# Seven half-block products for the second feed-forward product of nine token pairs

## The chip, the core and the metric

The kernel runs on one core of one Trainium2 chip. TensorE (PE in the profile; PEld is its weight load, which overlaps the matmuls) multiplies into eight PSUM banks; VectorE (DVE), ScalarE (ACT) and GpSimd (POOL) do the elementwise work; SyncE (SP) issues most DMAs. Each engine takes its instructions strictly in the order in which the program lists them for it and waits on semaphores for the others. The metric is the device time of one execution in microseconds. The kernel before took 181.5 us, the median of three runs (181.38 to 181.68).

## The reference

A gated outer-product recurrence runs over 768 time steps for 4 batches and 8 heads of width 48; its result, 3072 tokens of width 384, goes through a feed-forward layer of width 2048. All arrays are float32 outside the kernel.

```python
def _attn_ref(q, k, v, f_logit):                      # 4, 8, 768, 48
    f = 1.0 / (1.0 + np.exp(-f_logit))
    for t in range(S):
        state = f[:, :, t, :, None] * state + np.einsum('bhd,bhe->bhde', k[:, :, t], v[:, :, t])
        y[:, :, t] = np.einsum('bhd,bhde->bhe', q[:, :, t], state)

def _moe_ref(x, w_in, w_out):                         # 3072x384, 384x2048, 2048x384
    h = x @ w_in
    g = h * (1.0 / (1.0 + np.exp(-h)))
    return g @ w_out
```

## The kernel before

**Tiles.** The sequence is cut into chunks of 128 tokens, six for each batch, 24 in all. Two chunks form a pair (`PAIRS`). Pairs 0 to 3 (form T) hold the first two chunks of one batch, with even and odd tokens dealt to the two tiles; pairs 4 to 11 (form N) hold the same chunk of two batches.

**Tasks.** A pair goes through a fixed set of tasks, named by two or three letters. Loads `f`, `k`, `q`, `v` come through SP. `E` and `L` (ACT) take the logarithm of the gate, `cs` (PE) sums it over the chunk, `a`, `ia`, `al` (ACT) take exponentials of the sums. `qg` and `ki` (DVE or POOL, line 341) multiply q and k by them. They are transposed, either on PE (`tq`, line 348, and a copy `qkc`) or by a DMA from SP (`qkD`, line 360). `sc` (PE, lines 369 and 373) makes the scores, `at` (DVE, line 377) masks them, `y` (PE, lines 285, 385, 389) makes the chunk's result, `d`, `sd` and `su` (PE, DVE, POOL or DVE; lines 297, 406, 410, 420) carry the state to the next chunk. `yc` copies the result out of PSUM as bf16; it is transposed into `xT` on PE (`yT`, line 397, with the copy `xc`) or by DMA (`yD`, line 401).

**The feed-forward layer.** `mi` (line 271) is one of eight parts of the first product: two blocks of 128 of the 2048 columns, three matmuls of 256 token columns for each, with the weights of `w_in_sb` as the loaded operand. For pairs 0 and 1 each part is done for one chunk at a time, with matmuls of 128 columns. `si` (ACT, line 276) takes SiLU of a part into `hT`, bf16. `mo` (line 306) is one of four parts of the second product for one chunk: four matmuls of 384 columns that accumulate in one PSUM bank, with a block of `hT` as the loaded operand and `w_out_sb` streamed. A chunk needs 16 of them. Only pair 11 does them in two halves of 192 columns. `oc` (lines 185 and 187) copies the bank into `ob`, `so` (lines 316 and 318) stores it.

**Order.** A table, `PLAN`, lists every task with its engine and the buffer that it takes. The program is emitted in that order, so the table sets the order in every engine's queue, SP's included. `idle` tasks (line 465) are matmuls of zeros that nothing reads: they stand where PE would have nothing to do at the start. `SLOTS` gives the number of buffers of each kind: six each for k, q and v, and eight PSUM banks (`pb`) for all uses. A change of activation table (line 513) is inserted wherever ACT's next task needs another one.

Of the kernel before, what the change touches and what calls it, by code (L numbers as in the profile page):

```python
# [10 lines left out]
F32 = mybir.dt.float32  # L11
BF16 = mybir.dt.bfloat16
AF = mybir.ActivationFunctionType
PSUM = bass.MemoryType.PSUM
# [19 lines left out]
SLOTS = dict(f=4, k=6, q=6, v=6, e=2, lf=3, x=5, qk=5, vb=7, qkT=4, qkTT=2, atm=4, yb=3, xT=4, hT=4, sd=2, al=6, ob=6, pb=8, st0=1, st1=1, st2=1, st3=1)  # L34
# [15 lines left out]
mi.0.1.1:P:0 si.0.3:A:1 mi.0.1.0:P: mi.0.5.1:P: si.1.5:A: ki.3.0:G: mi.0.0.0:P:6 si.0.1:A: mi.0.6.0:P:5 mi.0.0.1:P: su.1.1:G:0 mi.0.7.1:P:4 si.0.0:A:  # L50
mi.0.7.0:P: si.0.2:A: mi.0.6.1:P: ki.3.1:G: mi.1.1.0:P: si.0.6:A: mi.1.7.0:P:0 tq.3.0:P:6 mi.1.7.1:P: qkc.3.0:A:1 mi.0.4.0:P:2 tq.3.1:P:5 si.1.7:A:
mi.0.4.1:P: f.4.0:S:1 mo.0.0.0:P:6 qkc.3.1:A: mo.0.1.0:P:0 si.1.1:A: mi.1.6.1:P:5 si.0.5:A: mi.1.6.0:P: si.1.2:A: mo.1.1.0:P:7 si.1.6:A: mo.0.1.1:P:
si.0.4:A: si.0.7:A: sc.3.1:P:3,1 sc.3.0:P:5,2 at.3.1.0:V:2 vb.2.0:A:4 mo.0.1.2:P: at.3.1.1:V: mo.1.1.1:P: at.3.0.0:V:3 mo.0.0.1:P: q.4.0:S:4
mo.0.1.3:P: vb.3.0:V:5 mo.1.1.2:P: vb.3.1:V:6 oc.0.1:V:0 mo.1.1.3:P: at.3.0.1:V: v.5.0:S:4 mo.0.0.2:P: vb.2.1:V:2 v.5.1:S: oc.1.1:V:1 d.2:P:4,3
so.1.1:G: y.2:P:1,5 su.2.0:V:0 v.4.0:S:5 d.3:P:0,2 E.4.0:A:0 sd.2.1:V:0 y.3:P:7,4 yc.3.0:V:1 yi.2.1:P: mo.1.0.0:P:3 L.4.0:A:1 yc.2.1:V:2 yT.3.0:P:7
su.3.0:V:0 mo.1.0.1:P: yc.2.0:V:0 v.8.1:S:0 mo.0.0.3:P: sd.3.1:V:1 yT.2.1:P:5 oc.0.0:A:2 cs.4.0:P:0 k.4.0:S:4 xc.2.1:V:2 yi.3.1:P: a.4.0:A:2 so.0.0:G:
mo.1.0.2:P: ia.4.0:A:1 q.4.1:S: xc.3.0:A:3 yT.2.0:P:1 mo.1.0.3:P: xc.2.0:V: E.5.0:A:1 k.6.1:S:5 mi.2.2:P:2 al.4.0:A:4 cs.4.1:P:6 mi.2.3:P:5 al.4.1:A:5
a.4.1:A:3 q.5.0:S:5 L.5.0:A:2 mi.2.7:P:7 k.5.1:S:0 yc.3.1:A:1 mi.2.4:P:1 ia.4.1:A:0 ki.4.0:G:1 q.5.1:S: mi.2.5:P:0 oc.1.0:A:3 vb.4.0:G:3 yT.3.1:P:4
mi.2.0:P:6 xc.3.1:V: su.2.1:G:0 mi.3.6:P:3 si.2.3:A:2 mi.3.1:P:4 qg.4.0:V: si.2.7:A: k.4.1:S: su.3.1:G:0 si.2.5:A: mi.3.7:P:5 si.3.1:A:3 f.6.0:S:2
mi.2.6:P:7 vb.5.1:A:0 si.3.7:A: d.4.0:P:0 v.4.1:S: mi.2.1:P:4 sd.4.0:V:0 si.2.6:A: qg.4.1:V:2 tq.4.0:P:5 si.2.4:A: mi.3.2:P:0 si.2.1:A: k.7.0:S:1  # L60
si.2.0:A: mi.3.0:P:7 ki.4.1:G: qkc.4.0:A:0 cs.5.1:P:1 mi.3.5:P:4 qkD.4.1:S:1 si.3.0:A: mo.2.1.0:P:6 si.2.2:A: si.3.5:A: sc.4.0:P:5,7 v.7.0:S:1
# [485 lines left out]
```

## Time and profile before

| | |
|---|---|
| device time, median of three runs | 181.5 us (181.38 to 181.68) |
| span of the profiled execution, first to last instruction | 179.2 us |
| PE busy | 170.5 us, 2042 matmuls |
| ACT busy | 132.7 us, 251 instructions |
| DVE busy | 79.7 us, 166 instructions |
| POOL busy | 61.6 us, 106 instructions |
| granted TensorE clock | 1.000 |
| HBM read and written | 25.17 MB and 4.72 MB |

The profile is one execution. The device time of that execution is not recorded apart; its span is 2.3 us shorter than the median, and those 2.3 us lie before the first and after the last instruction. "Busy" is the time in which at least one instruction of an engine runs. A group of instructions is shown with its line, engine, operation, the tiles that it writes and reads, its shape and its count, then its busy time, the mean duration of one, and the idle time of its engine just before it. The chain of waits starts at the last instruction and goes back, at each step, to what released it.

### The profile page before, as it was taken

The numbers are of one execution on the slowest core, as the hardware profiler recorded it, in microseconds if no ns is written. First come the engines' busy times: TensorE is split into PE (matmuls) and PEld (weight loads), VectorE is DVE, ScalarE is ACT, GpSimd is POOL, SyncE is SP. The second block draws the span as 40 slices with busy tenths as digits, with TensorE's granted clock in tenths as the row PEclk, the third lists the DMA queues.
The fourth block names the chain that finished last, engine by engine and source line by source line (L and its number), as shares of the span: only waits on it lengthen the run. The fifth ranks groups of instructions, "written<-read, shape, count | busy, mean of one in ns | idle before, by whom it ended". The sixth has DMA issues, their size and how long they took to land.

```text
span 179.2 us, 4981 instructions
## 1 busy us (share of the span) xinstructions
PE 170.5 (95%) x2042; PEld 129.0 (72%) x2044; DVE 79.7 (44%) x166; ACT 132.7 (74%) x251; POOL 61.6 (34%) x106
## 2 busy tenths in 40 slices
PE   6769989999999999999999999999999999999993
PEld 2345779975788866778678877875876786788782
DVE  7078994008821246456673703342335747500002
ACT  3989983895289999999967558988796991178410
POOL 6036995000274004554044170636303592000010
PEclk9999999999999999999999999999999999999999
DMA  6999999999999799998478998994994496320043
GB/s 159 324 325 325 240 204 207 199 187 190 242 230 212 92 208 221 168 241 144 84 145 170 188 210 141 252 263 103 179 251 94 97 190 215 88 70 0 0 150 117
DMA packets 109366, 31.91 MB, mean 178 GB/s; under 512 B 103536, under 2 KB 108768, under 8 KB 109344
## 3 DMA queue, kind: packets, MB, share of 16 engines
q1 hardware_dynamic: 104464, 25.60, 70.2%
q0 software_dynamic: 4880, 6.00, 15.7%
q8 instruction: 16, 0.26, 0.6%
q14 instruction: 6, 0.05, 0.1%
HBM read 25.17 MB, written 4.72 MB: 167 GB/s over the span
## 4 chain that ended last, share of the span: by engine, by line
PE 77%; ACT 9%; DVE 4%; DMA 3%; SPq 2%; issue 1%; POOL 1%; DVEq 0%
PE pb L306 32%; PE pb L271 32%; ACT hT L276 4%; DMA q<-in_q_dram 3%; PE pb L373 2%; SPq L241 2%; PE pb L385 2%; PE pb L348 2%; PE pb L389 2%; DVE qk L341 2%; ACT L513 1%; DVE atm L377 1%; PE pb L331 1%; PE pb L397 1%; DVE st L420 1%
## 5 line engine op out<-in xcount | busy, mean ns | idle before, releaser
L306 PE MATMUL pb<-w_out_sb,hT 128*128 128x384 bf16 (+1 forms) x416 | 70.4, 314 | 0.2 <-ACT hT L276 0.2
L271 PE MATMUL pb<-xT,w_in_sb 128*128 128x256 bf16 (+1 forms) x672 | 68.9, 257 | 0.0
L271 PEld LDWEIGHTS <-w_in_sb 128*128 128x128 bf16 x672 | 56.6, 98 | 7.5 <-issue 0.3
L276 ACT ACTIVATE hT<-pb 128x512 bf16<-128x512 f32 x96 | 51.8, 617 | 12.4 <-PE pb L271 12.0
L306 PEld LDWEIGHTS <-hT 128*128 128x128 bf16 x416 | 37.7, 98 | 18.7 <-ACT hT L276 0.4
L377 DVE TENSOR_TENSOR atm<-pb,triu 128x512 bf16<-128x512 f32 x32 | 20.6, 684 | 20.5 <-PE pb L373 17.8
L336 ACT ACTIVATE x<-pb 128x384 f32<-128x384 f32 x48 | 22.1, 508 | 1.5 <-PE pb L331 1.4
L420 POOL TENSOR_TENSOR st<-sd,al 48x192 bf16<-48x192 f32 x32 | 16.6, 518 | 18.7 <-PE pb L385 12.1
L341 POOL TENSOR_TENSOR qk<-q,x 128x384 bf16<-128x384 f32 x11 | 11.3, 1025 | 31.9 <-ACT x L336 14.5
L513 ACT ACT_TABLE_LOAD x15 | 19.2, 1283 | 0.3
L185 ACT COPY ob<-pb 128x384 f32<-128x384 f32 (+1 forms) x15 | 6.8, 453 | 12.6 <-PE pb L306 12.6
L377 DVE TENSOR_TENSOR atm<-pb,mask 128x512 bf16<-128x512 f32 x16 | 10.2, 685 | 12.4 <-ACT hT L276 11.1
L187 DVE COPY ob<-pb 128x384 f32<-128x384 f32 (+1 forms) x11 | 5.8, 535 | 22.2 <-PE pb L306 22.2
L318 POOL DMA_DIRECT2D out_dram<-ob x8 | 4.6, 578 | 28.4 <-ACT ob L185 24.8
L316 POOL DMA_DIRECT2D out_dram<-ob x14 | 7.6, 548 | 19.6 <-DVE ob L187 15.9
L341 DVE TENSOR_TENSOR qk<-q,x 128x384 bf16<-128x384 f32 x13 | 7.6, 593 | 13.7 <-ACT x L336 13.7
L248 ACT ACTIVATE e<-f 128x768 f32<-128x768 f32 (+1 forms) x13 | 10.4, 800 | 4.4 <-DMA f<-in_f_logit_dram 4.2
L410 DVE TENSOR_TENSOR sd<-pb,st 128x384 f32<-128x384 f32 x16 | 8.9, 554 | 10.6 <-PE pb L406 3.9
L341 POOL TENSOR_TENSOR qk<-k,x 128x384 bf16<-128x384 f32 x10 | 10.8, 1082 | 6.4 <-ACT al L278 2.0
L185 ACT CAST yb<-pb 128x384 bf16<-128x384 f32 x12 | 5.6, 479 | 9.7 <-PE pb L389 9.6
L341 DVE TENSOR_TENSOR qk<-k,x 128x384 bf16<-128x384 f32 x14 | 9.9, 710 | 0.9 <-ACT x L336 0.9
L187 DVE CAST yb<-pb 128x384 bf16<-128x384 f32 x12 | 6.6, 556 | 8.0 <-PE pb L389 5.9
(72 smaller groups left out, 157.4 us busy)
## 6 DMA issues: line engine op xcount, KB each, us to landing
f<-in_f_logit_dram SPq DMA_DIRECT2D x11, 384.0 KB, 4.7
q<-in_q_dram SPq DMA_DIRECT2D x16, 192.0 KB, 4.1
v<-in_v_dram SPq DMA_DIRECT2D x16, 192.0 KB, 3.9
k<-in_k_dram SPq DMA_DIRECT2D x16, 192.0 KB, 3.9
k<-in_k_dram SPq DMA_DIRECT2D x4, 384.0 KB, 4.8
v<-in_v_dram SPq DMA_DIRECT2D x4, 384.0 KB, 9.5
q<-in_q_dram SPq DMA_DIRECT2D x4, 384.0 KB, 4.9
w_in_sb<-in_moe_w_in_dram POOLq DMA_DIRECT2D x4, 384.0 KB, 9.5
```

The lines of the kernel that those rows point to most:

```text
L185: nc.scalar.copy(dst, src)
L187: ENG[eng].tensor_copy(dst, src)
L248: return nc.scalar.activation(e, at("f", P)[:, j * w:(j + 1) * w], AF.Exp, scale=-1.0)
L271: nc.tensor.matmul(h[:, i, cols], w_in_sb[:, kk, n * 128:(n + 1) * 128], at("xT", P)[:, kk, cols], start=(kk == 0), stop=(kk == KT - 1))
L276: return nc.scalar.activation(at("hT", P)[:, 2 * j:2 * j + 2, :], at("h", P, j).rearrange("p (n c) -> p n c", n=2), AF.Silu)
L306: nc.tensor.matmul(at("o", P, i)[:, cols], at("hT", P)[:, n, i * C:(i + 1) * C], w_out_sb[:, n, cols], start=(n == 0), stop=(n == NT - 1))
L336: nc.scalar.activation(at(kind, P, i).rearrange("p h d -> p (h d)"), at("cs", P, i)[:, 0:HD], AF.Exp, scale=1.0 if kind == "ia" else -1.0)
L341: ENG[eng].tensor_mul(at("qk", P, i)[:, j, :, 0:D], heads("qk"[j], P, i), at("ia" if j else "a", P, i))
L377: ENG[eng].tensor_mul(at("atm", P, i)[:, r], at(f"s{r}", P, i).rearrange("p (n c) -> p n c", c=C), mask[:, None, :].to_broadcast([C, NP, C]))
L410: nc.vector.tensor_add(at("sd", P, i), d_ps, prev_state(P, i))
L420: ENG[eng].tensor_mul(at("st", P, i)[lo:lo + D, :, r * D:(r + 1) * D], src[lo:lo + D, :, r * D:(r + 1) * D], al_of(P, i)[lo:lo + D, :, Non ...
L513: nc.scalar.preload_act_table_set(TABLES[mode])
```

## The change

**The second product.** For pairs 2 to 10 the product of the pair's 256 by 2048 block with the 2048 by 384 weights is split in half in all three directions and done by Strassen's scheme. `hT` is laid out chunk by chunk, so that its four blocks are (chunk, half of the 2048). The weights' four blocks are 1024 by 192.

- `wt`, five times in all: a sum or difference of two weight blocks, in bf16, on DVE (8 blocks of 192 columns, 1536 elements in each partition), into the new tiles `w_sum`.
- `hs`, four times for each pair, on DVE: sums and differences of blocks of `hT` in bf16. Numbers 1, 6 and 7 have 1024 elements in each partition, number 5 makes two sums at once and has 2048. Numbers 6 and 7 are written over a block of `hT`, number 1 into a free `qkT` buffer, number 5 into a free `qkTT` buffer.
- `ms`, seven times for each pair: eight matmuls of 192 columns. Numbers 2 to 5 go into the two halves of one PSUM bank, 6 and 7 into those of a second, 1 into half of a third.
- `cc`, `ca` and `oc`: seven of the nine `cc` copies and all 36 `ca` sums are on DVE, and of the nine `oc` copies four on DVE and five on ACT. `cc` copies a quarter out of PSUM, `ca` 0 and 1 add a quarter to it, `ca` 2 and 3 make the two diagonal quarters of the output from it, `oc` copies the two others.

Pairs 0, 1 and 11 keep the old product.

**Buffers.** k, q and v have four buffers each instead of six. The result of `E` is written over `f`, whose buffers `e` go away. `ob` holds a pair: four of them instead of six single ones. `qkT` has one buffer more.

**Order.** `PLAN` is new throughout. One pair of `tq`/`qkc` and one of `yT`/`xc` have become DMA transposes; 15 whole-chunk stores are on SP instead of 8, and 7 on POOL instead of 14 (the stores of a T pair are two DMAs each); 28 idle matmuls instead of 24, of which 21 in a row at the start instead of 11; 18 activation table loads instead of 16; on POOL one `qg` and one `ki` less and four `vb` more; on ACT four `vb` less.

```diff
-SLOTS = dict(f=4, k=6, q=6, v=6, e=2, lf=3, x=5, qk=5, vb=7, qkT=4, qkTT=2, ..., ob=6, pb=8, ...)
+SLOTS = dict(f=4, k=4, q=4, v=4, lf=3, x=5, qk=5, vb=7, qkT=5, qkTT=2, ..., ob=4, pb=8, ..., ct=2)
...
-f.2.0:S:0 k.0.0:S:0 f.0.1:S:1 f.0.0:S: E.2.0:A:0 f.1.0:S:2 L.2.0:A:0 v.1.0:S:0 q.0.0:S:0 idle.512.11::0 cs.2.1:P:0 ...
+f.2.0:S:0 f.0.1:S:1 f.0.0:S: f.1.0:S:2 v.0.0:S:0 q.0.0:S:0 E.2.0:A: E.0.1:A: L.2.0:A:0 k.0.0:S:0 L.0.1:A:1 idle.512.21::1 cs.2.1:P:0 ...
...
+    KH, W = NT // 2, d_model // 2
+    w_sum = {m: sb.tile([128, KH, W], BF16, name=f"w_sum{m}") for m in (1, 3, 4, 6, 7)}
...
+    BANK = {2: "oa", 3: "oa", 4: "oa", 5: "oa", 6: "ob2", 7: "ob2", 1: "oc"}
+    def h_sum(P, m):
+        if m == 5:
+            return at("hE", P).rearrange("p j n g s c -> p (j n g s c)").rearrange("p (u n c) -> p u n c", u=2, c=C)
+        if m == 1:
+            return at("hF", P).rearrange("p j n c -> p (j n) c")
+        return at("hT", P)[:, 1, 0:KH, :] if m == 6 else at("hT", P)[:, 0, KH:NT, :]
...
+        if kind == "wt":
+            blk = lambda r, c: w_out_sb[:, r * KH:(r + 1) * KH, c * W:(c + 1) * W]
+            x, y, op = {1: (blk(0, 0), blk(1, 1), ALU.add), 3: (blk(0, 1), blk(1, 1), ALU.subtract), 4: (blk(1, 0), blk(0, 0), ALU.subtract),
+                        6: (blk(0, 0), blk(0, 1), ALU.add), 7: (blk(1, 0), blk(1, 1), ALU.add)}[rest[0]]
+            return ENG[eng].tensor_tensor(out=w_sum[rest[0]], in0=x, in1=y, op=op)
+        if kind == "hs":
+            m = rest[1]
+            hT = at("hT", P)
+            blk = lambda u, k: hT[:, u, k * KH:(k + 1) * KH, :]
+            x, y, op = {6: (blk(1, 0), blk(0, 0), ALU.subtract), 7: (blk(0, 1), blk(1, 1), ALU.subtract), 1: (blk(0, 0), blk(1, 1), ALU.add),
+                        5: (hT[:, :, 0:KH, :], hT[:, :, KH:NT, :], ALU.add)}[m]
+            return ENG[eng].tensor_tensor(out=h_sum(P, m), in0=x, in1=y, op=op)
+        if kind == "ms":
+            m = rest[1]
+            hT = at("hT", P)
+            for n in range(KH):
+                if m == 3:
+                    x, w = hT[:, 0, n], w_sum[3][:, n]
+                elif m == 4:
+                    x, w = hT[:, 1, KH + n], w_sum[4][:, n]
+                elif m == 5:
+                    x, w = h_sum(P, 5)[:, 0, n], w_out_sb[:, KH + n, W:2 * W]
+                elif m == 2:
+                    x, w = h_sum(P, 5)[:, 1, n], w_out_sb[:, n, 0:W]
+                else:
+                    x, w = h_sum(P, m)[:, n], w_sum[m][:, n]
+                half = 1 if m in (2, 4, 6) else 0
+                first = n == 0 and m in (1, 3, 6, 7)
+                nc.tensor.matmul(at(BANK[m], P)[:, half * W:(half + 1) * W], x, w, start=first, stop=(n == KH - 1), skip_group_check=True)
+            return
+        if kind == "cc":
+            return copy(eng, at("ct", P), at("oa", P)[:, W:2 * W])
+        if kind == "ca":
+            ct = at("ct", P)
+            two = lambda x: x[:, 0:2 * W].rearrange("p (u w) -> p u w", w=W)
+            if rest[1] < 2:
+                return nc.vector.tensor_add(ct, at("oa", P)[:, 0:W] if rest[1] == 0 else at("oc", P)[:, 0:W], ct)
+            diag = at("ob", P).rearrange("p u (x w) -> p (u x) w", w=W)[:, 0:4:3, :]
+            if rest[1] == 2:
+                return nc.vector.tensor_sub(diag, ct[:, None, :].to_broadcast([C, 2, W]), two(at("oa", P)))
+            return nc.vector.tensor_add(diag, two(at("ob2", P)), diag)
...
-                e = at("e", P)[:, j * w:(j + 1) * w]
+                e = at("f", P)[:, j * w:(j + 1) * w]
...
-            return nc.scalar.activation(at("hT", P)[:, 2 * j:2 * j + 2, :], at("h", P, j).rearrange("p (n c) -> p n c", n=2), AF.Silu)
+            return nc.scalar.activation(at("hT", P).rearrange("p u n c -> p n u c")[:, 2 * j:2 * j + 2], at("h", P, j).rearrange("p (n u c) -> p n u c", n=2, u=2), AF.Silu)
```

**Three places where the order changes.** In the rows below a row names the line (of its own kernel), the operation, the tile written, the tiles read and the shape.

PE, near the end, where the products of pair 10 begin among the last `mi` of pair 11. Before (hT3 is pair 10's block, pb a PSUM bank):

```order
L306 MATMUL pb0_140<-w_out_sb_162,hT3_125 128x384
...
L271 MATMUL pb1_141<-xT3_121,w_in_sb_161 128x256
...
L306 LDWEIGHTS hT3_125
L306 MATMUL pb5_145<-w_out_sb_162,hT3_125 128x384
...
L306 MATMUL pb7_147<-w_out_sb_162,hT2_124 128x192
```

Now (hT1 is pair 10's block, hT3 pair 9's, qkT4 holds sum 1 of pair 10):

```order
L267 LDWEIGHTS hT1_116
L267 MATMUL pb5_136<-w_sum3_157,hT1_116 128x192
...
L267 MATMUL pb5_136<-w_sum4_158,hT1_116 128x192
...
L329 MATMUL pb1_132<-xT3_114,w_in_sb_154 128x256
...
L267 MATMUL pb3_134<-w_sum6_159,hT3_118 128x192
...
L267 MATMUL pb6_137<-w_sum1_156,qkT4_101 128x192
```

A chunk's sixteen matmuls of 384 columns into one bank have become runs of eight of 192 columns into halves of three banks, and products of two pairs stand among each other.

DVE, in the last third, from the masks of pairs 10 and 11 to the last copies. Before (the rows up to the end of DVE's list):

```order
L377 TENSOR_TENSOR atm_114<-pb_145,triu 128x512
L377 TENSOR_TENSOR atm_113<-pb_146,triu 128x512
L187 COPY ob_134<-pb_142 128x384
L187 CAST yb_116<-pb_144 128x384
L187 COPY ob_139<-pb_145 128x384
L187 COPY ob_137<-pb_140 128x384
L187 COPY ob_134<-pb_146 128x192
```

Now (hT_118 is pair 9's block, ct the running quarter of an output):

```order
L435 TENSOR_TENSOR atm_107<-pb_138,triu 128x512
L193 CAST yb_109<-pb_137 128x384
L250 TENSOR_TENSOR qkTT_102<-hT_118 128x2048
L275 TENSOR_TENSOR ct_143<-pb_136,ct_143 128x192
L278 TENSOR_TENSOR ob_130<-ct_143,pb_132 128x2x192
L250 TENSOR_TENSOR hT_118<-hT_118 128x1024
L275 TENSOR_TENSOR ct_144<-pb_134,ct_144 128x192
```

Where seven rows took DVE from the last masks to the end of its list, sums of blocks and of PSUM quarters now follow one another; masks and copies for `y` stand behind them in the same queue.

SP, at the very start. Before:

```order
L241 DMA f_61<-in_f_logit_dram 128x8x96
L241 DMA k_65<-in_k_dram 128x8x96
L241 DMA f_62<-in_f_logit_dram 128x4x96 x2
L241 DMA f_63<-in_f_logit_dram 128x8x96
L241 DMA v_77<-in_v_dram 128x8x96
L241 DMA q_71<-in_q_dram 128x8x96
```

Now:

```order
L299 DMA f_61<-in_f_logit_dram 128x8x96
L299 DMA f_62<-in_f_logit_dram 128x4x96 x2
L299 DMA f_63<-in_f_logit_dram 128x8x96
L299 DMA v_73<-in_v_dram 128x8x96
L299 DMA q_69<-in_q_dram 128x8x96
L299 DMA k_65<-in_k_dram 128x8x96
```

The first k goes from second to seventh DMA, and pair 0's gate and q each come one place earlier; the v that is loaded first is pair 0's and no longer pair 1's.

178 lines of the change are left out of this document (97 added, 81 removed).

## The prediction, made before the changed kernel had run

> **What bounds the kernel now.** I read the busy shares first, then the slices, the chain of waits, and two stretches by engine.
>
> ```profile
> PE 170.5 (95%) x2042; PEld 129.0 (72%) x2044; DVE 79.7 (44%) x166; ACT 132.7 (74%) x251; POOL 61.6 (34%) x106
> ...
> PE   6769989999999999999999999999999999999993
> ...
> DVE  7078994008821246456673703342335747500002
> ACT  3989983895289999999967558988796991178410
> ...
> PE 77%; ACT 9%; DVE 4%; DMA 3%; SPq 2%; issue 1%; POOL 1%; DVEq 0%
> ...
> 60.00:70.00 10.00, 9.97 (x102) 6.84 (x99) 3.70 (x7) 9.94 (x18) 2.01 (x3) 1.00 1.03 174
> ...
> 120.00:140.00 20.00, 20.00 (x194) 14.20 (x192) 6.79 (x13) 16.43 (x31) 6.51 (x9) 1.00 0.77 157
> ```
>
> The two last rows are stretches: length, then busy time and count of PE, PEld, DVE, ACT, POOL. From about 27 us to 176 us PE has no gap, and the chain lies on it for 77% of the span. ACT is full only around 50 to 80 us, beside a PE that is full too. DVE is 44% busy. Time is therefore PE's work plus what PE waits. What PE's pieces cost stands in the chain (start, us, piece):
>
> ```profile
> 35.00 0.67 PE pb L271 x12
> 35.67 0.45 PE pb L348 x8
> 47.87 0.17 PE pb L397 x3
> 115.57 0.17 PE pb L385 x4
> 115.74 0.20 PE pb L389 x8
> 120.52 5.20 PE pb L306 x32
> 141.32 5.24 PE pb L271 x48
> 163.73 0.33 PE pb L306 x4
> 166.67 9.52 PE pb L306 x88
> ```
>
> Back to back, a matmul of 384 columns takes 5.20/32 = 162.5 ns, of 256 columns 5.24/48 = 109 ns, of 192 columns (the piece of four is half a `mo` of pair 11) 0.33/4 = 82.5 ns, of 128 columns 0.67/12 = 56 ns. The last piece checks the third: by the order 28 of its 88 matmuls have 384 columns and 60 have 192, so (9.52 - 28 x 0.1625)/60 = 82.8 ns.
>
> **The change on PE.** Nine pairs gave up 9 x 32 = 288 matmuls of 384 columns, 46.8 us, for 9 x 56 = 504 of 192, 41.6 us: **-5.2 us**. One `tq` (0.45) and one `yT` (0.17) leave PE: **-0.6 us**; their DMA transposes go to SP.
>
> **The start.** What ran before the first score, in time order:
>
> ```profile
> 1.37 4.37 PE L465 MATMUL pb<-zero,triu 128*128 128x512 bf16 x11 [1.37 <-POOL triu masks.py:66]
> 4.92 0.84 ACT L260 ACTIVATE lf<-e 128x768 bf16<-128x768 f32 x1
> 5.82 0.48 PE L324 MATMUL pb<-lf,tincl 128*128 128x384 bf16 x2
> ...
> 5.24 4.81 DMA q<-in_q_dram
> ```
>
> Eleven idle matmuls ended as the first logarithm did, at 5.8 us. Twenty-one end later: the ten more at the 384-column pace (512/384 x 0.1625 = 0.217 us) take 2.2 us, to 7.9 us, while the logarithm, now behind half of another exponential, ends about 0.5 us later than before. So pair 0's cumulative sums start about 1 us late. Against that q is one transfer earlier than its 10.05 us, and ACT and DVE have fewer copies ahead of it; k, now the seventh transfer, lands about where q did. I charge **0**, with 1.5 us to either side. The end (last copy, last store) is unchanged: 0.
>
> **The change on DVE.** Durations by form (busy, mean ns):
>
> ```profile
> L377 DVE TENSOR_TENSOR atm<-pb,triu 128x512 bf16<-128x512 f32 x32 | 20.6, 684 | 20.5 <-PE pb L373 17.8 <-ACT hT L276 2.6
> L341 DVE TENSOR_TENSOR qk<-k,x 128x384 bf16<-128x384 f32 x14 | 9.9, 710 | 0.9 <-ACT x L336 0.9
> L410 DVE TENSOR_TENSOR sd<-pb,st 128x384 f32<-128x384 f32 x16 | 8.9, 554 | 10.6 <-PE pb L406 3.9 <-POOL st L420 3.1 <-PE pb L397 1.7
> L187 DVE COPY ob<-pb 128x384 f32<-128x384 f32 x10 | 5.4, 552 | 22.0 <-PE pb L306 22.0
> L187 DVE CAST vb<-v 128x384 bf16<-128x384 f32 x11 | 5.1, 482 | 0.0
> L187 DVE COPY qkTT<-pb 128x1024 bf16<-128x1024 bf16 x3 | 2.0, 680 | 0.0
> L187 DVE COPY xT<-pb 128x384 bf16<-128x384 bf16 x4 | 1.4, 353 | 4.8 <-PE pb L397 4.8
> L187 DVE COPY ob<-pb 128x192 f32<-128x192 f32 x1 | 0.4, 359 | 0.2 <-PE pb L306 0.2
> ```
>
> No row has a two-input bf16 sum from SBUF, so `hs` and `wt` are bounded from both sides. By slope of the float32 rows, (684 - 554)/128 = 1.02 ns an element, 1024 elements take 1.21 us, 1536 1.73, 2048 2.25. By that of the bf16 copies, (680 - 353)/640 = 0.51 ns, they take 0.68, 0.94 and 1.20 us. I take the lower, since the type is that of the copies, and keep the upper as a rival. [...]
>
> All nine pairs: `hs` 27 x 0.68 + 9 x 1.20 = 29.2 us, `wt` 5 x 0.94 = 4.7, `ca` 18 x 0.36 + 18 x 0.554 = 16.5, `cc` 7 x 0.36 = 2.5; the output copies come out about even, and two more `qg`/`ki` add 1.1. DVE goes from 79.7 to some 134 us. That fits the whole span, but not evenly. Between pair 1's last product and the fifth product of pair 9, counted in the changed order, PE has 51 `ms` (0.66 each), 51 `mi` (0.655) and, by the small pieces shown (0.37 for a `y`, 0.17 for a `d`, about 0.35 for one `sc` of eight), 16.4 us of others: 83.5 us. In the same stretch DVE has 30 masks x 0.644 (busy over count) = 19.3, 20 short and 7 long `hs` = 22.0, 28 `ca` = 12.6, 6 `cc` = 2.2, and 46 others (`sd`, `yc`, `qg`, `ki`, `oc`, `vb`, one `qkc`) = 25: 81 us. **So DVE needs 97% of PE's time for two thirds of the kernel.**
>
> On top comes GpSimd. These rows are VectorE's products with two SBUF inputs (minimum/median/maximum ns), and one of them in time order beside a POOL product:
>
> ```profile
> L341 DVE TENSOR_TENSOR qk<-k,x x14: 547/550/1359, 10.6 to 141.6; 128x384 bf16<-128x384 f32 x14
> L341 DVE TENSOR_TENSOR qk<-q,x x13: 542/549/1111, 10.1 to 141.2; 128x384 bf16<-128x384 f32 x13
> ...
> 11.44 1.06 POOL L341 TENSOR_TENSOR qk<-k,x 128x384 bf16<-128x384 f32 x1 [2.04 <-ACT al L278]
> 11.56 1.36 DVE L341 TENSOR_TENSOR qk<-k,x 128x384 bf16<-128x384 f32 x1
> ```
>
> The DVE product that met POOL's ended 0.42 us after it and took 0.8 us more than the median. The means (710, 593) lie above the medians by 14 x 0.16 + 13 x 0.04 = 2.8 us over 27 products, 0.1 us each. `hs` has two SBUF inputs as well: 42 such operations in the stretch cost 4.2 us more, 85.2 us in all, 1.7 us over PE. [...] I charge **+1.8 us** as PE waiting for DVE. Its lower bound is 0 (rows that stand back to back overlap a little), its upper bound is the first rival.
>
> What is queued behind a late `hs` on DVE: masks, then `y` on PE, and the copies that free PSUM banks; a pair's product now holds three banks instead of two.
>
> **Other parts.** ACT gains two table loads and loses seven copies of `ob`, four of `vb`, one `qkc` and one `xc`: 2 x 1.28 against about 3.4 + 2.2 + 1.0 + 0.5, so it becomes lighter by some 4 us; 0 on the path, PE being full beside it. POOL has two products of 1.03 less, four casts more and eight stores less: 0. These rows price them:
>
> ```profile
> L513 ACT ACT_TABLE_LOAD x15 | 19.2, 1283 | 0.3
> L185 ACT COPY ob<-pb 128x384 f32<-128x384 f32 x12 | 5.8, 486 | 4.9 <-PE pb L306 4.9
> L341 POOL TENSOR_TENSOR qk<-q,x 128x384 bf16<-128x384 f32 x11 | 11.3, 1025 | 31.9 <-ACT x L336 14.5 <-issue 9.6 <-DVE sd L410 7.6
> L420 POOL TENSOR_TENSOR st<-sd,al 48x192 bf16<-48x192 f32 x32 | 16.6, 518 | 18.7 <-PE pb L385 12.1 <-DVE sd L410 5.2
> ```
>
> **The sum.** 179.2 - 5.2 - 0.6 + 0 + 1.8 = 175.2 us of span; with the 2.3 us that lie around it, **177.5 us** against the median of 181.5.
>
> **Rivals.** *VectorE becomes the bound* (slower). POOL reads SBUF for 24 of the stretch's 83.5 us (12 `su` of two rows of 0.52, 9 products of 1.03 to 1.08, 4 casts of about 0.5). If each of the 42 two-input operations meets it that often (28%) at the full 0.8 us, DVE needs 81 + 9.5 = 90.5 us there, 7.0 more than PE: 179.2 - 5.8 + 7.0 + 2.3 = **182.7**. It is slower than before from 89.7 us of DVE on (83.5 + 5.8 + 0.4). For it: the 97%, and masks that feed PE from the same queue. Against it: most `hs` stand several PE parts ahead of their product in the order, and the mean excess was 0.1 us.
>
> *The sums run at the float32 pace* (slower). The stretch's `hs` take 20 x 1.21 + 7 x 2.25 = 40.0 instead of 22.0 us: 18 more, so 177.5 + 18, about **195**. Against it: bf16 copies run at twice that pace.
>
> *Loads and transposes late behind stores.* SP gets fourteen more store DMAs and two more transposes.
>
> ```profile
> SPq L318 <- DVE ob L187: 14.9, 3, 12.0
> ...
> 118.70 1.83 SPq L316 DMA_DIRECT2D out_dram<-ob  x2
> ...
> qkT<-qk SPq DMA_TRANSPOSE x14, 3.5
> ```
>
> At 0.9 us each they take SP some 15 us more, a store that waits for DVE has held SP for 12 us, and k, q and v can be fetched less far ahead. One transpose (3.5 us to landing) that PE then waits for gives 177.5 + 3.5 = **181.0**.
>
> *Weight loads bound the short matmuls* (slower).
>
> ```profile
> L306 PEld LDWEIGHTS <-hT 128*128 128x128 bf16 x416 | 37.7, 98 | 18.7 <-ACT hT L276 0.4
> ```
>
> If each of the 504 took its load's 98 ns, they would need 49.4 us, 7.8 more than charged: **185.3**. The 56 ns of twelve matmuls with a load each speak against it. [...]
>
> **How the numbers follow.** Forecast 0.58; VectorE the bound 0.22; SP late 0.11; float32 pace 0.06; weight loads 0.03. The forecast's own range is 175 (start 1 us better, no waiting) to 179.5. The range to hold the time 8 times in 10 is 175.0 to 183.5: below it 0.05, above it the float32 pace, the weight loads and a quarter of the first rival, 0.14. A difference of 0.2% is about what the spread of the runs before lets one tell from none. Faster: the forecast and half of SP late, 0.64. Same: 0.04 of SP late and 0.02 of the first rival, 0.06. Slower: 0.30.
>
> **What would show it.** `ms` at 82 ns a matmul in the chain, and PE busy of some 165 us. `hs` at about 0.7 and 1.2 us; at 1.2 and 2.25 the third case has come. DVE at 130 to 138 us, with full slices from 60 to 150 us; PE gaps there that end on DVE's masks or sums, 1 to 3 us in all by the forecast, 6 or more by the first rival. PE waiting for a DMA transpose would mean SP. First scores later than 15.5 us would make the start's 0 wrong.

## The result, and the profile after

The changed kernel took **186.6 us** (median of four runs, 185.3 to 186.8) against 181.4 us before: 1.0259 times as long, 95% interval 1.0216 to 1.0303. The forecast was 177.5 us. The profiled execution took 186.75 us, its span was 185.0 us. Here and below a median is over all executions, while a ratio leaves out those that ran slow, at a lower clock throughout or more than 1.5% above the fastest of their kernel.

The page of the profile after: busy times, slices, the chain's shares, and three groups.

```profile
PE 169.2 (91%) x2253; PEld 144.5 (78%) x2253; DVE 125.2 (68%) x252; ACT 130.7 (71%) x240; POOL 54.7 (30%) x94
...
PE   7996989999999999989949959999986999999992
...
DVE  6159973574668888789946493997949589907340
...
PEclk9999999999999999999987988999999999999999
...
PE 60%; DMA 11%; ACT 10%; SPq 7%; DVE 5%; issue 4%; POOL 1%; DVEq 0%; POOLq 0%; ACTq 0%
...
L329 PE MATMUL pb<-xT,w_in_sb 128*128 128x256 bf16 (+1 forms) x672 | 73.2, 262 | 4.6 <-DMA xT<-yb 3.9
...
L250 DVE TENSOR_TENSOR qkTT<-hT 128x2048 bf16<-128x2048 bf16 x9 | 11.0, 1218 | 6.4 <-ACT hT L334 6.4
...
L250 DVE TENSOR_TENSOR hT<-hT 128x1024 bf16<-128x1024 bf16 x18 | 12.3, 690 | 0.1
```

PE's row, all nines from 27 us on before, now has a 4 at 92 us, a 5 at 106 us and a 6 at 139 us (a slice is 4.6 us), and the clock has two dents, from 92 to 102 us and from 106 to 116 us. DMA and SP's queue together, 5% of the chain before, are 18%. DVE is less busy than forecast, and its long sums take what was put for them. The holes by name, from the order of time on PE (start, length, group, idle before it and what ended that):

```profile
79.83 1.47 PE L329 MATMUL pb<-xT,w_in_sb 128*128 128x256 bf16 x12 [0.74 <-ACT hT L334]
95.64 1.00 PE L431 MATMUL pb<-qkT 48*128 48x128 bf16 x16 [2.71 <-DMA qkT<-qk]
108.42 5.76 PE L329 MATMUL pb<-xT,w_in_sb 128*128 128x256 bf16 x36 [2.19 <-DMA xT<-yb]
137.75 0.40 PE L431 MATMUL pb<-qkT 48*128 48x128 bf16 x8 [0.89 <-DMA qkT<-qk]
142.90 1.48 PE L329 MATMUL pb<-xT,w_in_sb 128*128 128x256 bf16 x12 [1.69 <-DMA xT<-yb]
```

They add up to 8.2 us; from 27 us on there is no other wait of PE over 0.2 us. Four of the five end on a DMA transposition, none on a sum of VectorE. The third row shows a second loss: 36 matmuls of 256 columns took 5.76 us, 160 ns each, where 109 ns was the pace before. The stretches around it (length; PE, PEld, DVE, ACT, POOL; granted clock; DMA share; GB/s):

```profile
108.00:111.00 3.00, 2.58 (x17) 2.02 (x18) 3.00 (x6) 0.06 (x1) 0.00 (x0) 0.73 0.92 179
111.00:114.00 3.00, 3.00 (x21) 2.31 (x20) 1.48 (x3) 1.14 (x3) 0.00 (x0) 0.70 1.08 209
114.00:117.00 3.00, 3.00 (x45) 2.44 (x43) 1.17 (x2) 2.91 (x6) 0.00 (x0) 1.00 1.01 222
```

The 0.73 and 0.70 are means over three microseconds. The trace's records of the granted clock say more exactly: 0.50 from 109.36 to 112.78 us and 1.00 on either side, and likewise 0.50 from 95.71 to 99.12 us, behind the first long hole. Each is a stretch of 3.41 us at half speed, which costs 1.7 us of TensorE's work. What makes a transposition late is best seen in the chain of waits of the same kernel (start, length, what lay on the chain):

```profile
122.46 0.67 PE pb L267 x8
123.34 0.62 SPq L374
124.00 0.59 SPq L374
124.70 1.27 SPq L418
126.02 1.26 SPq L459
...
131.25 0.79 SPq L376
132.08 1.85 DMA out_dram<-ob
133.94 3.77 DMA qkT<-qk
137.75 0.42 PE pb L431 x8
```

For ten microseconds, from 123.3 to 133.9 us, the chain does not touch PE: it goes from command to command through SP's queue, stores (lines 374 and 376), transpositions (418, 459) and loads. Then the transposition that PE needs is issued and takes 3.8 us.

### The profile page after: what moved, and what is told of

The parts are those of the page before. It is cut to its first block, busy times and chain, and to the rows that moved or that the text cites. A ratio compares the mean times of both kernels' runs of the same rounds, so it can differ in the third digit from the quotient of the medians.

```text
span 185.0 us, 5495 instructions
## 1 busy us (share of the span) xinstructions
PE 169.2 (91%) x2253; PEld 144.5 (78%) x2253; DVE 125.2 (68%) x252; ACT 130.7 (71%) x240; POOL 54.7 (30%) x94
## 4 chain that ended last, share of the span: by engine, by line
PE 60%; DMA 11%; ACT 10%; SPq 7%; DVE 5%; issue 4%; POOL 1%; DVEq 0%; POOLq 0%; ACTq 0%
PE pb L329 27%; PE pb L267 13%; PE pb L364 6%; DMA qkT<-qk 5%; PE pb L533 4%; DMA xT<-yb 3%; DVE atm L435 3%; ACT L581 3%; ACT hT L334 3%; SPq L299 3%; DMA v<-in_v_dram 2%; ACT x L394 2%; SPq L418 2%; PE pb L431 2%; SPq L374 1%
## 5 line engine op out<-in xcount | busy, mean ns | idle before, releaser
L329 PE MATMUL pb<-xT,w_in_sb 128*128 128x256 bf16 (+1 forms) x672 | 73.2, 262 | 4.6 <-DMA xT<-yb 3.9
L267 PE MATMUL pb<-w_sum,hT 128*128 128x192 bf16 x288 | 29.2, 246 | 0.0
L267 PEld LDWEIGHTS <-hT 128*128 128x128 bf16 x288 | 23.7, 98 | 0.7
L364 PE MATMUL pb<-w_out_sb,hT 128*128 128x384 bf16 (+1 forms) x128 | 18.6, 286 | 0.0
L267 PE MATMUL pb<-w_out_sb,qkTT 128*128 128x192 bf16 x144 | 15.5, 253 | 0.1
L250 DVE TENSOR_TENSOR qkTT<-hT 128x2048 bf16<-128x2048 bf16 x9 | 11.0, 1218 | 6.4 <-ACT hT L334 6.4
L364 PEld LDWEIGHTS <-hT 128*128 128x128 bf16 x128 | 11.2, 98 | 2.6
L267 PEld LDWEIGHTS <-qkTT 128*128 128x128 bf16 x144 | 12.5, 100 | 0.7 <-issue 0.4
L306 ACT ACTIVATE f<-f 128x768 f32<-128x768 f32 (+1 forms) x13 | 10.4, 809 | 2.8 <-DMA f<-in_f_logit_dram 2.8
L250 DVE TENSOR_TENSOR hT<-hT 128x1024 bf16<-128x1024 bf16 x18 | 12.3, 690 | 0.1
L533 PE MATMUL pb<-zero,triu 128*128 128x512 bf16 x28 | 9.3, 498 | 1.4 <-POOL triu masks.py:66 1.4
```

Of the source, the lines that this page charges most:

```text
L250: return ENG[eng].tensor_tensor(out=h_sum(P, m), in0=x, in1=y, op=op)
L267: nc.tensor.matmul(at(BANK[m], P)[:, half * W:(half + 1) * W], x, w, start=first, stop=(n == KH - 1), skip_group_check=True)
L306: return nc.scalar.activation(e, at("f", P)[:, j * w:(j + 1) * w], AF.Exp, scale=-1.0)
L329: nc.tensor.matmul(h[:, i, cols], w_in_sb[:, kk, n * 128:(n + 1) * 128], at("xT", P)[:, kk, cols], start=(kk == 0), stop=(kk == KT - 1))
L364: nc.tensor.matmul(at("o", P, i)[:, cols], at("hT", P)[:, i, n], w_out_sb[:, n, cols], start=(n == 0), stop=(n == NT - 1))
L533: nc.tensor.matmul(buf["pb", int(got)][:, 0:rest[0]], triu, zero[:, 0:rest[0]], start=True, stop=True, skip_group_check=True)
```

## The experiments

Medians throughout; ratios, with their 95% intervals, are to the kernel before on the same chip (181.3 to 181.7 us).

**e1: stores off SP.** The seven stores of T pairs that the change put on SP, 14 DMAs, go back to POOL's queue, at the same places.

```diff
-so.0.0:S: ... so.0.1:S: ... so.3.1:S: ... so.1.0:S: ... so.1.1:S: ... so.2.1:S: ... so.2.0:S:
+so.0.0:G: ... so.0.1:G: ... so.3.1:G: ... so.1.0:G: ... so.1.1:G: ... so.2.1:G: ... so.2.0:G:
```

> The changed kernel with the seven whole-chunk stores of the T pairs (fourteen DMAs) issued by POOL instead of SP, at the same places of the table. Theory SP (SP's queue is full from 70 to 140 us, so DMA transposes and loads leave it late and PE waits for them): SP is 9 to 14 us lighter between 95 and 133 us, the gaps after 100 us shrink, time 181 to 185. Theory DVE (VectorE's sums make PE late): 186.6, unchanged within 0.5. Theory BUF (four buffers for k, q, v instead of six let the loads start late): 185.5 to 186.6.

Measured 180.1 us (178.1 to 182.6), 0.9873 [0.979, 0.9957]: 6.5 us less than the changed kernel and now below the kernel before. From its page and its order of time on PE:

```profile
PE 166.0 (93%) x2253; PEld 142.5 (80%) x2253; DVE 126.0 (71%) x252; ACT 130.8 (73%) x240; POOL 62.7 (35%) x108
```

```profile
94.03 0.62 PE L430 MATMUL pb<-qkT 48*128 48x128 bf16 x16 [1.30 <-DMA qkT<-qk]
...
105.00 4.09 PE L328 MATMUL pb<-xT,w_in_sb 128*128 128x256 bf16 x36 [1.61 <-DMA xT<-yb]
...
136.16 1.48 PE L328 MATMUL pb<-xT,w_in_sb 128*128 128x256 bf16 x12 [0.54 <-DMA xT<-yb]
```

The same holes, smaller (4.3 us with the others from 27 us on that are over 0.2 us and wait for an engine or a DMA), and the same 36 matmuls at 4.09 us, at full clock. PE's busy time falls by 3.2 us with not one matmul fewer: that much of it had been clock, two stretches of 1.7 us. The transposition behind the first hole is issued before any T store, so its shrinking from 2.71 to 1.30 us isn't the stores' doing: the same wait is 1.41 us in e13, with the stores on SP, and 2.09 us in e11, without them. Some 3 us of the difference between these two profiles, this hole and its clock, are therefore not to be put down to the stores; but the 6.5 us are the difference of the medians, and a repetition (e16, below) gives 180.2 us again. Nor do the stores hold SP by waiting for their data: in the changed kernel's list of SP's waits none belongs to a T store.

**e8: the reverse.** The same seven stores of the kernel before go from POOL to SP, everything else as before.

```diff
-so.1.1:G: ... so.0.0:G: ... so.2.0:G: ...
+so.1.1:S: ... so.0.0:S: ... so.2.0:S: ...
```

> The kernel before with its seven T-pair stores that POOL issues (fourteen DMAs) issued by SP at the same places of the table. If such stores on SP are enough by themselves: 183 to 187, with PE gaps that end on transposes. If they harm only beside loads that come just in time (four buffers, new order): 181.4 to 182.3.

Measured 184.0 us, 1.0141 [1.0115, 1.0166]: 2.7 us more. From 27 us on its one hole over a microsecond ends on a transposition:

```profile
128.32 0.83 PE L270 MATMUL pb<-xT,w_in_sb 128*128 128x256 bf16 x6 [1.52 <-DMA xT<-yb]
```

So the stores on SP cost either kernel time, the changed one more. That this is for want of PE work that covers the transpositions is argued below.

**e2 and e10: no sums on VectorE.** The sums of `hs` and `wt` are left out, in e2 from the changed kernel, in e10 from e1.

```diff
-            return ENG[eng].tensor_tensor(out=w_sum[rest[0]], in0=x, in1=y, op=op)
+            return
-            return ENG[eng].tensor_tensor(out=h_sum(P, m), in0=x, in1=y, op=op)
+            return
```

> The changed kernel without the sums of hT blocks and of weight blocks: the 63 half-block products read the unsummed blocks, so the output is another one. VectorE loses 29 + 4.7 us of work, everything else stands. Theory DVE: 180 or less, since VectorE is then far from PE's work. Theories SP and BUF: 185 to 187, since no load, store or transpose moves.

> As e1 (the stores of pairs 0 to 3 on POOL), and with all sums of weight and activation blocks left out, so that each product takes a block as it stands; what is left out is 42 operations, 31 us of VectorE. If VectorE holds TensorE up by the 1.8 us that the prediction put for it, this comes to 178 us against e1's 180.1. If the sums cost nothing once SP is free, 180 us. If they cost as much as their removal was worth with the stores on SP, 2.4 us, 177.7 us.

e2: 184.2 us, 1.0108 [1.0039, 1.0178], 2.4 us less than the changed kernel. The page and the order of time on PE:

```profile
PE 166.9 (91%) x2253; PEld 143.0 (78%) x2253; DVE 94.6 (51%) x211; ACT 130.7 (71%) x240; POOL 52.9 (29%) x94
```

```profile
94.44 0.62 PE L423 MATMUL pb<-qkT 48*128 48x128 bf16 x16 [2.52 <-DMA qkT<-qk]
...
104.48 0.40 PE L423 MATMUL pb<-qkT 48*128 48x128 bf16 x8 [1.76 <-DMA qkT<-qk]
...
107.16 5.76 PE L321 MATMUL pb<-xT,w_in_sb 128*128 128x256 bf16 x36 [1.52 <-DMA xT<-yb]
...
141.88 1.48 PE L321 MATMUL pb<-xT,w_in_sb 128*128 128x256 bf16 x12 [2.09 <-DMA xT<-yb]
```

With 31 us taken from VectorE the kernel is still slower than before, and its waits on transpositions are at least as long in sum. The time lies between the two expectations, and the runs do not show where the 2.4 us come from; in the profiles e2 has one stretch at half clock where the changed kernel has two, which is 1.7 us. e10: 180.9 us (177.9 to 181.6), 0.9858 [0.9771, 0.9945], against e1's 180.1 us: nothing that can be told from zero, though a spread of some 4 us would hide one or two. **VectorE is not what made the kernel slower.**

**e3 and e7: the old product in the new order.** Pairs 2 to 10 get `mo` back where `ms` stood, without sums; in e3 the stores stay on SP, in e7 they are on POOL as in e1. In e3 some banks and output buffers are overwritten before their last reader has read them; in e7, where the copies `oc` of pairs 5, 6 and 7 stand in another order, they are not.

```diff
-hs.4.5:V:1 ... ms.4.3:P:0 ... ms.4.4:P: ... cc.4:V:0 ... ca.4.0:V: ... ms.4.2:P: ...
+mo.4.0.0:P:0 ... mo.4.0.1:P: ... mo.4.0.2:P: ...
```

> The changed kernel with the old second product for pairs 2 to 10 (matmuls of 384 columns at the places of the half-block products, two copies for each pair, no sums), in the new order, with the new buffers, stores and loads. PE's work is 5.2 us more, VectorE's some 50 us less. If the new order and its loads and transposes are the cause: 186 to 190. If the half-block scheme itself is (sums, three banks for each pair, weight loads): 181 to 183.

> The old second product in the new order, as before, but with the T pairs' stores on POOL. What the half-block scheme is worth where SP holds PE less: PE's work is 5.2 us more than in the changed kernel with the stores on POOL, so 183 to 185.5 if PE bounds both; 180 to 181 if both are bound by transposes or the sums take back what the products give.

e3: 185.3 us, 1.0191 [1.0127, 1.0254]. e7: 183.9 us, 1.0125 [1.0091, 1.0159]. Its page, and its longest wait in the order of time on PE:

```profile
PE 171.3 (94%) x2037; PEld 128.9 (71%) x2037; DVE 84.3 (46%) x177; ACT 130.4 (72%) x238; POOL 60.3 (33%) x108
```

```profile
104.13 4.09 PE L324 MATMUL pb<-xT,w_in_sb 128*128 128x256 bf16 x36 [1.09 <-DMA xT<-yb]
```

Against e1, the half-block products take 171.3 - 166.0 = 5.3 us off PE's busy time and 3.8 us off the time. With the stores on SP they bring nothing (185.3 and 186.6 us), and with the old product the stores on SP cost only 1.4 us (e3 and e7). And e7 is some 2.5 us slower than the kernel before, with the same product and its T stores on POOL: the rest of the new order has a price of its own. Its trace shows most of it: from 27 us on PE waits 3.1 us, 2.3 of them for transpositions into `xT`, where the kernel before has no wait over 0.2 us.

**e4 and e9: four input buffers in the kernel before.** In e4 all loads keep their place, and the load of v for pair 11 overwrites a buffer that pair 8 has still to read. In e9 that load stands behind the last reader; there the table takes only four buffers of each kind in turn and leaves the two others unused. The edit of e4:

```diff
-SLOTS = dict(f=4, k=6, q=6, v=6, ...)
+SLOTS = dict(f=4, k=4, q=4, v=4, ...)
```

> The kernel before with four buffers each for k, q and v instead of six, taken in turn, in its own order. Theory BUF: 183 to 187, since SP's loads wait for buffers and hold the transposes behind them. Theories SP (its stores) and DVE: 181.4 to 182.

> The kernel before with four instead of six input buffers for k, q and v, in turn; one load, v of pair 11, is issued behind the last reader of the buffer it takes, all other loads keep their place. If the fewer buffers are a cause, loads wait on SP for the conversions that read a buffer and hold up the transposes behind them: over 1 us above before, up to 183 or 184 us. If they are none, the readers are done when the load's turn comes on SP: within 0.5 us of before's 181.4 us.

e4: 181.3 us, 0.9987 [0.9968, 1.0005]. e9: 182.0 us, 1.0024 [1.0002, 1.0045]. Fewer buffers cost about 0.4 us.

**e5 and e6: lighter or reordered SP.** To e1, e5 adds that the loads of v for pairs 6 to 11 are issued by POOL (H in the table); e6 that eleven loads with time to spare stand behind one or more transpositions on SP that they stood ahead of (its expectation speaks of fifteen). One place of each:

```diff
-v.6.1:S:2 ... v.6.0:S: ... v.7.1:S:3 ...
+v.6.1:H:2 ... v.6.0:H: ... v.7.1:H:3 ...
```

```diff
-k.8.1:S:1 ... yD.5.1:S:0
+yD.5.1:S:0 k.8.1:S:1
```

> The changed kernel with the T pairs' stores on POOL and also the twelve loads of v for pairs 6 to 11 issued by POOL, at the same places of the table. Theory SP (its full queue sends transposes late): the three gaps that are left (1.3, 1.6 and 0.5 us before a transposed tile) go, 176 to 179. Rival POOL (a load that waits for its buffer on POOL holds the state updates behind it): 181 or more, with PE gaps that end on POOL. Theory DVE: 180, no change.

> The changed kernel with the T pairs' stores on POOL, and on SP fifteen loads of k, q and v that are used more than 11 us of PE work later moved behind the next transposes. SP issues as much as before, in another order. Theory SP in the form that what counts is what stands ahead of a transpose: 177 to 179.5. In the form that SP's whole work counts: 180, as with the stores on POOL alone.

e5: 184.4 us, 1.013 [1.0069, 1.0191]. e6: 187.1 us, from 180.8 to 214.4, too scattered for a ratio. Neither gains what was hoped for: a shorter or reordered SP queue is not enough. e5's time is that of its rival (181 us or more), but its profile, taken at a clock of 0.855, has no wait that ends on POOL. In e6's profile the wait for `qkT` before 96.9 us is 3.40 us, longer than the changed kernel's 2.71, and one of 1.47 us ends on a state update of POOL. That loads which come through POOL, or later, are then late for `qg`, `ki` and `vb` at the head of the same chain is likely, but not shown.

**e11: five more stores off SP.**

```diff
-so.5.1:S: ... so.5.0:S: ... so.7.0:S: ... so.6.1:S: ... so.6.0:S:
+so.5.1:G: ... so.5.0:G: ... so.7.0:G: ... so.6.1:G: ... so.6.0:G:
```

> As e1, with the five stores of pairs 5, 6 and 7 that are left on SP between 100 and 145 us given to POOL too. If each command on SP's queue is what counts, these five are worth a further 1 to 2 us: 178 to 179 us against e1's 180.1, and the gaps before products that wait for transpositions shrink below e1's 3.7 us. If what is left after e1 is something else (clock, the transpositions' own landing time, POOL's own lateness), 180 us or above.

181.4 us (178.4 to 183.4), 0.9863 [0.98, 0.9925]: no gain over e1 that can be told. So not every command on SP counts.

**e12: work of PE moved ahead of the waits.**

```diff
-sc.7.1:P:3,4 ... sc.7.0:P:2,6 ms.4.5:P: ... mi.5.4:P:1
+ms.4.5:P: mi.5.4:P:1 sc.7.1:P:3,4 ... sc.7.0:P:2,6
-mi.7.6:P:2 ... mi.6.6:P:4
+mi.6.6:P:2 mi.7.6:P:0
-mi.10.2:P:4 ... y.11.0:P:6 ... ms.8.6:P:
+y.11.0:P:4 ms.8.6:P: mi.10.2:P:7
```

> As e1, with five pieces of TensorE's work moved ahead of the three products that wait longest for a DMA transposition (sc of pair 7, mi of pair 7, mi of pair 10): two pieces of half-block products, one group of the first product of pair 6 and of pair 5 each, and y of pair 11, 0.4 to 1.5 us of work that is ready before. If the late transpositions are the whole of what is left, their gaps (1.30, 1.61 and 0.54 us in e1) go to below 0.7 us each and the time falls by about 2 us to 178 us. If work moved only delays what depends on it, 180 us as e1 or more.

179.4 us (178.6 to 181.7), 0.9862 [0.9822, 0.9902], not to be told from e1. In the order of time on PE the wait for `qkT` is gone and that for `xT` is longer than e1's:

```profile
104.19 4.09 PE L328 MATMUL pb<-xT,w_in_sb 128*128 128x256 bf16 x36 [1.82 <-DMA xT<-yb]
```

Moved work has shifted the wait along the chain from `sc` to `y` to `mi`.

**e13 and e15: the number of commands, or their bytes?** e13 writes each T chunk of the changed kernel with one command instead of two. e15 leaves 14 commands on SP, of one row each, and sends the other rows from POOL.

```diff
-                for j in range(2):
-                    ENG[eng].dma_start(out=dst.rearrange("(p j) n -> j p n", j=2)[j], in_=ob[j * HC:(j + 1) * HC])
+                ENG[eng].dma_start(out=dst.rearrange("(p j) n -> j p n", j=2), in_=ob)
```

```diff
-                    ENG[eng].dma_start(out=dst...[j], in_=ob[j * HC:(j + 1) * HC])
+                    nc.sync.dma_start(out=dst...[j, 0:1], in_=ob[j * HC:j * HC + 1])
+                    ENG[eng].dma_start(out=dst...[j, 1:HC], in_=ob[j * HC + 1:(j + 1) * HC])
```

> The changed kernel, with the store of each chunk of pairs 0 to 3 written as one DMA of 128 rows in place of two of 64: 7 commands on SP in place of 14, with the same bytes, at the same places. If the number of commands on SP's in-order queue is what makes the loads and transpositions behind them late, about half of the 6.5 us that e1 brought comes back: 183 us against the changed kernel's 186.6. If it is the bytes, or the waiting of the stores for their sums, nothing does: 186 to 187 us. If one command of 128 rows takes SP as long as two of 64, the same.

> As e1, but SP keeps 14 store commands at their old places, each of a single row of 1.5 KB; the other 63 rows of each go out from POOL. SP has as many commands as in the changed kernel, and its queue almost none of their bytes. If the commands themselves, their issue time and their waits, delay what is behind them, the time is near the changed kernel's 186.6 us, with waits for DMA transpositions of 5 us or more in sum. If it is the stores' bytes ahead of the transpositions in the same queue (as the one-command stores of e13 suggest, whose 128 packets ran two at a time for 4.4 us), it is near e1's 180 us.

> e1 again, on the same chip as e15, as its measure: 178 to 182 us.

e13: **203.3 us**, 1.1178 [1.1134, 1.1222], with half the commands and the same bytes. In order of time on PE, then on SP:

```profile
104.97 5.27 PE L329 MATMUL pb<-xT,w_in_sb 128*128 128x256 bf16 x24 [6.97 <-DMA xT<-yb]
...
142.18 1.44 PE L329 MATMUL pb<-xT,w_in_sb 128*128 128x256 bf16 x6 [6.87 <-DMA xT<-yb]
```

```profile
92.94 1.70 SPq L373 DMA_DIRECT2D out_dram<-ob  x2
94.74 2.57 SPq L458 DMA_TRANSPOSE xT<-yb  x1
97.36 1.12 SPq L299 DMA_DIRECT2D q<-in_q_dram  x1
98.67 5.93 SPq L417 DMA_TRANSPOSE qkT<-qk  x1
```

The last transposition shown held SP for 5.93 us; the single ones of the changed kernel from 98 to 134 us hold it for 1.2 to 2.2 us. In the trace's packet records the 128 packets of 1.5 KB of such a store ran 2.1 at a time over 4.4 us; in the changed kernel those of a chunk stored by two commands ran, in one such place, 9.3 at a time over 1.1 us. The two stores' packets ran from 95.15 to 104.02 us, and SP was done with the transposition at 104.60. That it waited until those packets were through fits, but rests on this one place. Why the packets of the one command ran so few at a time was not shown.

e15: 183.5 us, 1.0106 [1.0079, 1.0132], beside 180.2 us for e1 repeated on that chip (e16; 0.99 [0.9838, 0.9962]). With all fourteen commands on SP and nearly none of their bytes, about half the loss is back (3.3 of 6.4 us). The first four of these commands in SP's order of time, in the changed kernel and in e15:

```profile
95.03 2.87 SPq L374 DMA_DIRECT2D out_dram<-ob  x4
```

```profile
91.22 2.29 SPq L373 DMA_DIRECT2D out_dram<-ob  x4
```

A command of one row still takes SP 0.57 us here, one of 64 rows 0.72; all fourteen take it 7.8 us in e15 and 10.0 in the changed kernel. **The commands alone bring back about half of the loss.** The other half goes with the other 63 rows, which take SP these 2.2 us more and put their packets on its queue; the two aren't told apart. In e15's profile the loss sits in one place: the wait for `xT` before the 36 matmuls, 1.61 us in e1, is 4.46 us there.

**e14: three transpositions taken off the DMA.** To e1: `yD` of pair 7, both, and of pair 10, the second, become transpositions on PE with a copy; two pieces of work are moved ahead of `sc` of pair 7 as in e12.

```diff
-yD.7.0:S:2 ... yD.7.1:S: ... yD.10.1:S:
+yT.7.0:P:0 xc.7.0:A:2 yT.7.1:P:1 xc.7.1:V: ... yT.10.1:P:5 xc.10.1:A:
```

> As e1, with the three transpositions of xT that have the least TensorE work between their issue and their first product (both of pair 7, the second of pair 10) done on TensorE with a copy from PSUM on ACT or VectorE, and two pieces of work moved ahead of sc of pair 7 as in e12. TensorE gets 9 transpositions of 128x128 more, about 0.5 us. If late DMA transpositions are what is left, the gaps of 1.61 and 0.54 us before mi of pairs 7 and 10 go, the others shrink since SP has three commands fewer, and the time falls by 2 to 3 us from e1's 180.1, to 177 to 178. If the gaps reappear at the next transposition, 179 to 180.

**178.2 us** (176.5 to 183.5, and one at 192.8), 0.9768 [0.9718, 0.9817]: faster than both kernels. In its profile PE's waits over 0.2 us from 27 us on add up to 0.5 us; but its granted clock is 0.85, PE is busy for 183.8 us and covers more, so this isn't compared with e1's 4.3 us.

## Why the prediction was wrong

**The step that failed** is the sum's 0 for SP's queue and the transpositions in it. The forecast held no wait of PE for a DMA. The rival *Loads and transposes late behind stores* named the mechanism, but it had a chance of 0.11 and a price of one exposed transposition, 3.5 us. It is what happened, and the stores alone cost 6.5 us (e1). The prediction had counted 15 us more of commands on SP and then asked for one late transposition; it should have asked how many stand among those commands (19 between 60 and 140 us) and how much PE work lies between each and its reader. It also priced only the wait. Two of the waits were paid a second time in clock: PE's busy time was 3.2 us above e1's. For the two profiled executions the balance comes out: 5.8 us less work as forecast, 8.2 us more of waits and an estimated 3.4 us more by the clock (two stretches of 3.41 us at half speed) make 5.8 us, and the span went from 179.2 to 185.0 us.

**Order, +2.5 us instead of 0.** The prediction put nothing for the rest of the new order except the start. e7 with the old product shows 2.5 us; of this the fewer buffers are 0.4 (e9). The rest is mostly the same mechanism: e7 waits 2.3 us for transpositions into `xT`, and 0.8 us for a SiLU of ACT. Why they are late there without the T stores on SP wasn't taken apart; two more DMA transpositions and loads nearer to their use are candidates, only argued.

**The product, -5.2 us on PE.** Right: 5.3 us by e7 and e1, with 84 ns a matmul (the chain's row at 122.46 us: eight in 0.67 us). Of this, 3.8 us reach the time. The shorter product takes cover from the transpositions: e1 waits 4.3 us from 27 us on where e7 waits 3.1.

**VectorE, +1.8 us.** Too much by the changed kernel's trace: from 27 us on no wait of PE over 0.2 us ends on a sum. e10 agrees, but its spread could hide the 1.8. The sums' pace was right (0.69 and 1.22 us against 0.68 and 1.20). DVE's busy time is 125 us instead of 134, mostly because its rows overlap: the busy times of its groups by form add up to 136 us. And the products beside POOL were shorter than before (0.61 and 0.57 us on average after 0.71 and 0.59), not longer. The rival built on that contention falls; the one on the float32 pace falls by the sums' pace, the one on weight loads by the 84 ns.

**The start, 0.** Right to half a microsecond: the first score came at 15.09 us, within the 15.5 that was set, and at 14.59 us before.

**The sum again**, by runs: 181.4 before; +2.5 order and buffers (e7); -3.8 product (e1); +6.5 stores on SP (the changed kernel): 186.6 us. It closes by construction, since each step is a difference of medians, and the steps depend on their order, as e3 shows: with SP loaded, the product brings nothing.

## What to carry to other kernels

A queue that issues just-in-time transpositions can be a bound of its own, as SP's was here (6.5 us for fourteen stores, e1): for each transposition, count what stands ahead of it in the queue, commands and bytes, and the work of the reading engine between issue and use. When a change makes that engine faster, the same order has less cover (e1 waits 4.3 us where e7, with the longer product, waits 3.1), so give the tightest transfers an engine that has time before counting the gain: stores to another queue (180.1 us in e1 after 186.6), transpositions to PE (178.2 us in e14, which also moves two pieces of work). And price a hole on TensorE with its clock, here 1.7 us for each stretch of 3.41 us at a clock of 0.50.

## What the runs showed of the hardware

**In these traces the granted clock changed in stretches of 3.41 us, and whether it fell after a hole went with the hole's share of a stretch.** In the clock records of all the traces here that start at full clock, a drop before the end of PE's work is to 0.50 and lasts 3.41, 6.83 or 10.24 us: one, two or three stretches. The records at full clock are whole numbers of them too: 88.75, 10.24 and 71.68 us in the changed kernel, 26, 3 and 21 stretches. From e16 and e12, order of time on PE and what follows:

```profile
103.53 5.76 PE L328 MATMUL pb<-xT,w_in_sb 128*128 128x256 bf16 x36 [1.92 <-ACT hT L333]
```

```profile
106.00:109.00 3.00, 3.00 (x22) 2.41 (x21) 0.62 (x2) 0.99 (x3) 0.00 (x0) 0.75 1.06 212
```

```profile
107.00:110.00 3.00, 3.00 (x43) 2.41 (x42) 0.00 (x1) 2.92 (x6) 0.00 (x0) 1.00 1.10 221
```

After 1.92 us the 36 matmuls took 5.76 us, with the clock at 0.50 from 104.08 to 107.50 us; after e12's 1.82 us, 4.09 us at 1.00. But a hole's length does not decide: e2's 2.52 and 2.09 us show no drop. What fits all of them is the share of a stretch in which PE was idle, by its own rows. The clock fell after stretches idle for 56% (e16), 61% (e11), 64 and 80% (the changed kernel), 64% (e2), 67% (e6) and more; it stayed after 55 and 53% (e13), 49% (the changed kernel's 1.69 us), 47% (e1's 1.61 us) and 41% (e12, where 1.41 of the 1.82 us fell on one stretch). The ends of PE's rows are modelled, so 55% and 56% are too close to set a border between them. e2's 2.52 us fell on two stretches, 48% of one and 26% of the next; its 1.52 us, with part of the 1.76 us ahead of it, made 64% of one and a drop. A stretch at 0.50 that was busy throughout was followed by 1.00; one that was idle for 28% or more (e6, e13, e15) by another at 0.50. So, by these runs, whether a hole of about two microseconds cost 1.7 us more (5.76 instead of 4.09 us for the same 36 matmuls) depended on where it fell.

**A T chunk's store in one command ran its packets 2.1 at a time**, 4.4 us for 192 KB (e13); in one place of the changed kernel two commands moved the same bytes in 1.1 us, 9.3 packets at a time. Why was not shown.
